# Layer one's output weights on one core: storing the converted value, or its two halves

## The chip, the core and the metric

The program runs on one core of one Trainium2 chip. The metric is device time in microseconds (us) of one execution. All inputs are float32, except that three weight arrays arrive as the words of float64 values and are converted on the chip.

## The reference

```python
# attention: 4 x 8 heads, 576 positions, head size 64, causal window 128, linear bias
scores = scale * np.matmul(q, k.transpose(0, 1, 3, 2))
scores = np.where(mask, scores + bias[None], -1000000000.0)
...
x = attn_out                                  # 2304 tokens x 512
# layer one, 1536 hidden units
g = x @ w_gate
x = (g * sigmoid(g) * (x @ w_val)) @ w_out    # the change concerns w_out here
# layer two, 2048 hidden units
h = x @ w_in
y = (h * np.tanh(softplus(h))) @ w_out
```

## The kernel before

TensorE multiplies in a format narrower than float32, so each operand is kept as two halves: `hi`, a copy rounded to that format (ScalarE, `hi_act`, L121), and `lo`, the rest (VectorE, `lo_dve`, L124). A product is three matmuls: hi by hi, hi by lo, lo by hi.

**Layer one** runs over five chunks of tokens (512, 384, 512, 512, 384). While chunk `ci` goes through layer one, the attention of chunk `ci+1` is mixed in. Per chunk there are 12 blocks `i` of 128 hidden units: `gv_groups` (L651) makes the gate and value products and the halves `hh`, `hl` of the activation, and `out_group` (L684) multiplies those by the block's output weights into four PSUM accumulators `acc0` to `acc3` (`proj`, L628: 12 matmuls). In the first four chunks `out_group` runs one block behind `gv`; in the last chunk (number 4) six behind, so that its last six output groups stand one after another at the end of layer one, with no other matmul between them.

**The ring.** The output weights come in six pieces `r` of two blocks. A piece lies as a tile `ring` [128, 2, 1024] (both halves, 1 MB); there are two such buffers, so piece r can enter only when the output groups of piece r-2 have been multiplied. In chunk 0 `conv_ring` (L489) converts a piece from float64 words (`convert`, L416), keeps the converted float32 value in a tile `cw` (512 KB), stores that to device memory (`w1od`), and makes the two halves. Chunks 1 to 4 call `load_ring` (L506), 24 times in all: it loads the float32 value back into a `cw` buffer and makes the halves again, one ScalarE and one VectorE instruction.

**Background.** Conversions, splits and loads are steps in a queue `bg`; `pump` issues some after every group. `conv_w2` (L520) converts layer two's weights in chunks 1 to 3 and spaces its blocks by a `pause` that it works out from the number of calls. In chunk 4 `combos` (L561) splits eight blocks of layer two's second weights and stores 1.8 MB for each.

**Layer two** starts on TensorE right after layer one's last output group. Its tokens are split into parts `xs1` to `xs7` (VectorE and ScalarE, from `xr`), and for each block j of two hidden tiles `make_win` (L817) makes a weight tile `win`: GpSimd forms four differences into a single buffer `t4` (L822), ScalarE the hi part, VectorE the lo part, in two instructions each, one from the raw block `w4` and one from `t4`. `hidden` (L833) multiplies seven groups of six matmuls per block j in the order 1, 6, 7, 5, 2, 4, 3; group 2 goes on in the bank of group 1, and group 3 in that of group 5. `bank()` (L712) gives the groups alternately a rotating bank and one of `acc0` to `acc3`; group 1 of the first block gets a rotating one and group 6 `acc1`. Layer one's results leave the accumulators through `evacuate` (L635): `acc0` and `acc2` by ScalarE (L638), `acc1` and `acc3` by VectorE (L639), into tiles `ev`.

**Order.** TensorE's order is the order of the program. On the other engines and in SyncE's DMA queue a scheduler sets the order when the kernel is built; each then runs strictly in that order.

Of the kernel before, what the change touches and what calls it, by code (L numbers as in the profile page):

```python
# [9 lines left out]
F32 = mybir.dt.float32  # L10
# [12 lines left out]
NF1, NF2 = F1 // 128, F2 // 128  # L23
# [69 lines left out]
def body(ctx: ExitStack, tc: tile.TileContext, qT, kT, vP, w1, w1o, w2, cst, yT):  # L93
    nc = tc.nc
# [4 lines left out]
    hp_ = sa.enter_context(tc.tile_pool(name="hp", bufs=2, side="right"))  # L99
    dr = ctx.enter_context(tc.tile_pool(name="dr", bufs=1, space=bass.MemoryType.DRAM))  # L100
    ps = ctx.enter_context(tc.tile_pool(name="ps", bufs=4, space=bass.MemoryType.PSUM))

    x2d = dr.tile([128, CT, NT], F32, name="x2d")
    w1od = dr.tile([NF1 // 2, 128, 1024], F32, name="w1od")
    w2d = dr.tile([NF2, 128, 1024], F32, name="w2d")
    w2o = dr.tile([7, 128, NJ, 2, 256], F32, name="w2o")
    cst_sb = const.tile([128, 452], F32, name="cst_sb")
# [12 lines left out]
    def hi_act(out, in_):  # L120
        return nc.scalar.activation(out=out, in_=in_, func=AF.Copy)  # L121

    def lo_dve(out, in_, hi):
        return nc.vector.tensor_tensor(out=out, in0=in_, in1=hi.bitcast(F32), op=ALU.subtract)  # L124
# [175 lines left out]
    last_of = {}  # L300
    behind = []
# [87 lines left out]
    wt, ring, spill = {}, {}, {}  # L389
    bg = collections.deque()  # L390
# [17 lines left out]
    def steps(key, fs, front=False):  # L408
        if front:
            bg.extendleft([(key if f is fs[-1] else None, f) for f in fs][::-1])  # L410
            return
        for f in fs[:-1]:
            bg.append((None, f))
        bg.append((key, fs[-1]))
# [36 lines left out]
    def halves(st, alloc, put):  # L451
        def f1():
            st["h"] = alloc()
            hi_act(st["h"][:, 0], st["w"])

        def f2():
            lo_dve(st["h"][:, 1], st["w"], st["h"][:, 0])
            put(st["h"])

        return [f1, f2]  # L460
# [4 lines left out]
    def ring_tile():  # L465
        return hp_.tile([128, 2, 1024], F32R, tag="ring", name="ring", bufs=2)

    stage = {}
# [20 lines left out]
    def conv_ring(r):  # L489
        st = {}  # L490

        def spill_it():
            nc.sync.dma_start(out=w1od[r], in_=st["w"])

        def put(w):
            ring[0, r] = w
            stage.pop(("o", r))
            if r + 1 < NF1 // 2:
                stage_other(("o", r + 1), w1o[r + 1])

        steps(
            ("ring", 0, r),
            convert(stage["o", r], st) + [spill_it] + halves(st, ring_tile, put),
        )

    def load_ring(ci, r):  # L506
        st = {}

        def f0():
            st["w"] = hp_.tile([128, 1024], F32, tag="cw", name="cw")  # L510
            nc.sync.dma_start(out=st["w"], in_=w1od[r])

        def put(w):
            ring[ci, r] = w

        steps(
            ("ring", ci, r), [f0, lambda: None] + halves(st, ring_tile, put), True
        )

    def conv_w2(blocks, calls):  # L520

        pause = max(6, (calls - 24 - 9 * len(blocks)) // len(blocks))

        def wait(n):
            for _ in range(n):
                bg.append((None, lambda: None))

        def block(i, after):
            st, raw = {}, {}

            def run(k):
                if not raw:
                    raw["f"] = convert(stage.pop(("2", i)), st)
                raw["f"][k]()

            def put():
                nc.sync.dma_start(out=w2d[i], in_=st["w"])

            for k in (0, 2, 3):
                bg.append((None, lambda k=k: run(k)))  # L540
                wait(1)
            if after is not None:
                bg.append((None, lambda: stage_other(("2", after), w2[after])))
            bg.append((None, lambda: run(1)))
            bg.append((None, lambda: run(4)))
            bg.append((None, put))
            wait(pause)

        bg.append((None, lambda: stage_other(("2", blocks[0]), w2[blocks[0]])))
        wait(pause)  # L550
        for i, after in zip(blocks, blocks[1:] + [None]):
            block(i, after)
# [406 lines left out]
    with tc.manual_schedule(engines={mybir.EngineType.PE}):  # L959
# [45 lines left out]
        for ci, p in enumerate(plansA):  # L1005
# [36 lines left out]
            for gi, (kind, i, f) in enumerate(groups):  # L1042
                if ci == 0 and kind == "gv" and gi % 3 == 0:
                    if 0 < i < NF1 - 2:
                        conv_w1(i + 2)
                    if i == 0:
                        conv_ring(1)
                        bg.insert(len(bg) - 4, (None, lambda: behind.append(last_of["x", 3])))
                f()
                if ci or not win:  # L1050
                    pump(CFG["pump_g"])
                elif gi % 3 == 0:
                    due = max(1, -(-len(bg) // 4))
                if not ci:
                    pump(due)
                while win and (spent * ng < (gi + 1) * total or gi == len(groups) - 1):
                    _, cost, e = win.popleft()
                    e()
                    spent += cost
                    pump(CFG["pump_p"] if ci else due)  # L1060
# [76 lines left out]
```

## Time and profile before

| | |
|---|---|
| median of 3 runs | 956.66 us (956.12 to 958.75) |
| the profiled execution | 955.31 us |
| its span in the trace | 953.4 us |
| TensorE busy | 924.4 us, 97% of the span |
| VectorE busy | 702.4 us, 74% |
| ScalarE busy | 524.5 us, 55% |
| GpSimd busy | 204.9 us, 21% |
| DMA queue of SyncE | 173.94 MB, 55.4% of 16 engines' span |

In the profile PE is TensorE, DVE VectorE, ACT ScalarE, POOL GpSimd and SP SyncE. A busy TensorE hides little: a microsecond taken from another engine shortens the run only where TensorE waits for that engine. The places where it waits are therefore what to look for, and the clock it is granted after each wait.

### The profile page before, as it was taken

What the parts mean: (1) busy time and instruction counts of PE and PEld (TensorE: products, weight loads), DVE (VectorE), ACT (ScalarE), POOL (GpSimd) and SP (SyncE); (2) the same over time, 40 slices, a digit from 0 to 9 for tenths busy, and PEclk for the clock granted to TensorE, in tenths of its full rate; (3) what the DMA queues carried; (4) which work ended last, traced back from release to release, by engine and by line L of the source; (5) the groups of instructions that cost most, each with busy time, mean ns of one, the idle gap of its engine ahead of it and who ended that gap; (6) DMA issues with size and microseconds to landing.
All of it is one profiled execution on the core that took longest, in us unless ns stands there. A gap on an engine that the chain in (4) does not pass through costs nothing. (4 is left out here: it accounts for less than half of the span.)

```text
span 953.4 us, 14622 instructions
## 1 busy us (share of the span) xinstructions
PE 924.4 (97%) x5040; PEld 832.0 (87%) x5040; DVE 702.4 (74%) x1341; ACT 524.5 (55%) x1135; POOL 204.9 (21%) x332
## 2 busy tenths in 40 slices
PE   6998999999999999999999998999999999999998
PEld 4766777899988888888889998899999999999997
DVE  6899997687866866567565668788877878677673
ACT  6766667666575655445534445555545555355442
POOL 0314223110210332010113325542012420132000
PEclk9999999999999999999999999999999999999999
DMA  9855434376636554165348993525793257830385
GB/s 305 294 202 197 167 91 126 97 228 198 216 94 202 167 186 134 51 206 168 132 147 284 375 327 101 210 70 193 252 307 110 77 184 261 301 118 4 103 266 183
DMA packets 76921, 174.86 MB, mean 183 GB/s; under 512 B 9136, under 2 KB 52528, under 8 KB 67120
## 3 DMA queue, kind: packets, MB, share of 16 engines
q1 hardware_dynamic: 76848, 173.94, 55.4%
q8 instruction: 40, 0.66, 0.3%
q14 instruction: 33, 0.27, 0.1%
HBM read 138.25 MB, written 35.65 MB: 182 GB/s over the span
## 5 line engine op out<-in xcount | busy, mean ns | idle before, releaser
L114 PE MATMUL g_ps<-xt,w 128*128 128x512 f32 (+1 forms) x1440 | 317.4, 373 | 0.6 <-DVE t L661 0.6
L114 PEld LDWEIGHTS g_ps<-xt,w 128*128 128x128 f32 x1440 | 257.7, 188 | 36.4 <-issue 2.3
L114 PE MATMUL bk<-xs,win 128*128 128x384 f32 x1008 | 180.1, 338 | 5.5 <-DVE G L726 4.9
L114 PEld LDWEIGHTS bk<-xs,win 128*128 128x128 f32 x1008 | 176.0, 189 | 9.2 <-DVE G L726 8.0
L114 PE MATMUL bk<-op,wout 128*128 128x384 f32 x1008 | 175.8, 335 | 0.6 <-DMA wout<-w2o 0.6
L114 PEld LDWEIGHTS bk<-op,wout 128*128 128x128 f32 x1008 | 174.8, 188 | 1.1 <-issue 1.1
L114 PE MATMUL acc<-hh,ring 128*128 128x512 f32 (+1 forms) x480 | 151.6, 379 | 1.9 <-DVE ring L124 1.8
L121 ACT ACTIVATE op<-G 128x768 fp32r<-128x768 f32 x84 | 70.8, 846 | 65.6 <-PE bk L114 63.0
L114 PEld LDWEIGHTS acc<-hh,ring 128*128 128x128 f32 x480 | 91.4, 193 | 15.2 <-DVE ring L124 2.6
L268 POOL TENSOR_SCALAR_AFFINE_SELECT PT<-PT 128x256 f32<-128x256 f32 (+4 forms) x80 | 51.8, 662 | 240.3 <-ACT PT L265 240.1
L124 DVE TENSOR_TENSOR op<-G,op 128x768 fp32r<-128x768 f32 x84 | 79.6, 955 | 26.9 <-ACT op L121 26.3
L822 POOL TENSOR_TENSOR t<-w 128x256 f32<-128x256 f32 x48 | 43.3, 921 | 224.6 <-DVE win L124 206.3
L114 PE MATMUL acc<-hl,ring 128*128 128x512 f32 (+1 forms) x240 | 90.2, 376 | 0.8 <-DVE hl L124 0.8
L237 ACT ACTIVATE Pt<-Pt,sm 128x128 f32<-128x128 f32 (+1 forms) x160 | 62.4, 391 | 17.1 <-DVE sm L233 16.1
L726 DVE TENSOR_TENSOR G<-u,bk 128x384 f32<-128x384 f32 x72 | 39.0, 553 | 31.8 <-PE bk L114 29.7
L121 ACT ACTIVATE hh<-t 128x512 fp32r<-128x512 f32 (+1 forms) x60 | 35.0, 583 | 47.0 <-DVE t L669 46.8
L1081 ACT ACTIVATE G<-G 128x384 f32<-128x384 f32 x72 | 36.8, 519 | 42.2 <-DVE G L726 42.2
L660 ACT ACTIVATE t<-g_ps 128x512 f32<-128x512 f32 (+1 forms) x60 | 32.7, 546 | 45.8 <-PE g_ps L114 45.6
L661 DVE SCALAR_TENSOR_TENSOR t<-t,g_ps 128x512 f32<-128x512 f32 (+1 forms) x60 | 37.6, 626 | 27.0 <-ACT t L660 26.9
L252 ACT ACTIVATE Pt<-Pt,sm 128x128 f32<-128x128 f32 (+1 forms) x144 | 46.3, 391 | 12.4 <-DVE sm L248 12.2
L114 PEld LDWEIGHTS acc<-hl,ring 128*128 128x128 f32 x240 | 46.3, 193 | 6.2 <-DVE hl L124 1.1
L124 DVE TENSOR_TENSOR hl<-t,hh 128x512 fp32r<-128x512 f32 (+1 forms) x60 | 39.8, 663 | 15.2 <-ACT hh L121 14.6
(78 smaller groups left out, 1235.1 us busy)
## 6 DMA issues: line engine op xcount, KB each, us to landing
wout<-w2o SPq DMA_DIRECT2D x42, 1024.0 KB, 6.1
wraw<-w SPq DMA_DIRECT2D x16, 1024.0 KB, 5.8
w2o<-chl SPq DMA_DIRECT2D x16, 896.0 KB, 9.0
wst<-w SPq DMA_DIRECT2D x12, 1024.0 KB, 6.9
cw<-w1od SPq DMA_DIRECT2D x24, 512.0 KB, 4.3
w<-w2d SPq DMA_DIRECT2D x24, 512.0 KB, 3.3
w2d<-cw SPq DMA_DIRECT2D x16, 512.0 KB, 5.0
wraw<-w1o SPq DMA_DIRECT2D x6, 1024.0 KB, 5.1
```

The lines of the kernel that those rows point to most:

```text
L114: nc.tensor.matmul(out=out, lhsT=lhsT, rhs=rhs, start=start, stop=stop, skip_group_check=True)
L121: return nc.scalar.activation(out=out, in_=in_, func=AF.Copy)
L124: return nc.vector.tensor_tensor(out=out, in0=in_, in1=hi.bitcast(F32), op=ALU.subtract)
L237: nc.scalar.activation(out=Pt[:q.qn], in_=Pt[:q.qn], func=AF.Exp, scale=-1.0, bias=sm[:q.qn, i:i + 1], accum_out=sm[:q.qn, 8 + i:9 + i],)
L252: last_of["exp"] = nc.scalar.activation(out=pt, in_=pt, func=AF.Copy, scale=r)
L268: nc.gpsimd.affine_select(out=here, in_=prev, pattern=[[0, m], [1, n]], compare_op=ALU.is_ge, fill=0.0, base=0, channel_multiplier=-1,)
L660: tanhs.append(nc.scalar.activation(out=t[:, :n], in_=st["g"][:, :n], func=AF.Tanh, scale=0.5))
L661: nc.vector.scalar_tensor_tensor(out=t[:, :n], in0=t[:, :n], scalar=1.0, in1=st["g"][:, :n], op0=ALU.add, op1=ALU.mult)
L726: nc.vector.tensor_tensor(out=out, in0=a, in1=b, op=op)
L822: nc.gpsimd.tensor_tensor(out=x[:, o], in0=a, in1=b, op=ALU.subtract)
L1081: nc.scalar.activation(out=out, in_=in_, func=AF.Mish)
```

## The change

The DRAM array takes both halves of a piece. `conv_ring` stores the finished ring tile after its lo half, in place of the float32 value after the conversion. `load_ring` becomes one step with one DMA of 1 MB straight into the ring tile; its ScalarE and VectorE instructions and its `cw` buffer go. The spacing of `conv_w2` and the place of one inserted step are adapted to the shorter queue.

```diff
-    w1od = dr.tile([NF1 // 2, 128, 1024], F32, name="w1od")
+    w1od = dr.tile([NF1 // 2, 128, 2, 1024], F32, name="w1od")
...
     def conv_ring(r):
         st = {}
 
-        def spill_it():
-            nc.sync.dma_start(out=w1od[r], in_=st["w"])
-
         def put(w):
             ring[0, r] = w
+            nc.sync.dma_start(out=w1od[r], in_=w.bitcast(F32))
             stage.pop(("o", r))
...
-            convert(stage["o", r], st) + [spill_it] + halves(st, ring_tile, put),
+            convert(stage["o", r], st) + halves(st, ring_tile, put),
...
     def load_ring(ci, r):
-        st = {}
-
         def f0():
-            st["w"] = hp_.tile([128, 1024], F32, tag="cw", name="cw")
-            nc.sync.dma_start(out=st["w"], in_=w1od[r])
-
-        def put(w):
-            ring[ci, r] = w
-
-        steps(
-            ("ring", ci, r), [f0, lambda: None] + halves(st, ring_tile, put), True
-        )
+            ring[ci, r] = ring_tile()
+            nc.sync.dma_start(out=ring[ci, r].bitcast(F32), in_=w1od[r])
+
+        steps(("ring", ci, r), [f0], True)
 
     def conv_w2(blocks, calls):
 
-        pause = max(6, (calls - 24 - 9 * len(blocks)) // len(blocks))
+        pause = max(6, (calls - 7  - 10 * len(blocks)) // (len(blocks) + 1))
...
-                        bg.insert(len(bg) - 4, (None, lambda: behind.append(last_of["x", 3])))
+                        bg.insert(len(bg) - 3, (None, lambda: behind.append(last_of["x", 3])))
```

TensorE's order stays as it was. The scheduler's order of the other engines changes in many places; three matter here.

The first is VectorE at the passage from layer one to layer two. `win_6106`, `win_6117` and `win_6220` are the weight tiles of blocks 0, 1 and 2 of layer two before; `w4` is a raw block and `t4` GpSimd's differences. Before:

```order
L124 TENSOR_TENSOR ring_6174<-cw_6172,ring_6174 128x1024
L124 TENSOR_TENSOR win_6117<-w4_6082,win_6117 128x768
L124 TENSOR_TENSOR xs7_6075<-xr_5421,xs7_6075 128x768
L726 TENSOR_TENSOR xr_5421<-xr_5421 128x2x384
L124 TENSOR_TENSOR win_6106<-t4_6074,win_6106 128x1024
L124 TENSOR_TENSOR xs6_6079<-xr_5421,xs6_6079 128x768
L124 TENSOR_TENSOR win_6220<-w4_6111,win_6220 128x768
L639 COPY ev_6201<-acc1_5765 128x384
L124 TENSOR_TENSOR xs3_6081<-xr_5421,xs3_6081 128x768
L639 COPY ev_6205<-acc3_5767 128x384
L124 TENSOR_TENSOR win_6117<-t4_6074,win_6117 128x1024
L726 TENSOR_TENSOR u_6235<-u_6235,bk_6237 128x384
```

The same place in the changed kernel, where blocks 0, 1 and 2 have the tiles `win_6037`, `win_6048` and `win_6148`:

```order
L124 TENSOR_TENSOR win_6048<-w4_6013,win_6048 128x768
L124 TENSOR_TENSOR win_6037<-t4_6005,win_6037 128x1024
L124 TENSOR_TENSOR xs3_6012<-xr_5364,xs3_6012 128x768
L124 TENSOR_TENSOR win_6148<-w4_6042,win_6148 128x768
L124 TENSOR_TENSOR win_6048<-t4_6005,win_6048 128x1024
L630 COPY ev_6129<-acc1_5716 128x384
L630 COPY ev_6133<-acc3_5718 128x384
L124 TENSOR_TENSOR win_6148<-t4_6005,win_6148 128x1024
L717 TENSOR_TENSOR u_6163<-u_6163,bk_6165 128x384
L717 TENSOR_TENSOR u_6180<-u_6163,bk_6173 128x384
L717 TENSOR_TENSOR G_6155<-u_6180,bk_6182 128x384
```

The ring instructions are gone. The evacuations of `acc1` and `acc3` (now L630) stood ahead of block 1's lo part from `t4`, and stand behind it; block 2's stood behind the first `u` and `G`, and stands ahead of them.

The second is SyncE's DMA queue at the same passage. `cw<-w1od` (before) and `ring<-w1od` (now) bring pieces 4 and 5 of the last chunk, `w4<-w2d` layer two's raw blocks. Before:

```order
L511 DMA cw_6063<-w1od_73 128x1024
L591 DMA w2o_75<-chl_5885 128x7x256
L591 DMA w2o_75<-chl_5888 128x7x256
L511 DMA cw_6172<-w1od_73 128x1024
L591 DMA w2o_75<-chl_5928 128x7x256
L591 DMA w2o_75<-chl_5949 128x7x256
L815 DMA w4_6072<-w2d_74 128x1024
L815 DMA w4_6082<-w2d_74 128x1024
L815 DMA w4_6111<-w2d_74 128x1024
```

Now, with piece 3 at the top:

```order
L507 DMA ring_5903<-w1od_73 128x2048
L582 DMA w2o_75<-chl_5819 128x7x256
L582 DMA w2o_75<-chl_5840 128x7x256
L806 DMA w4_6003<-w2d_74 128x1024
L806 DMA w4_6013<-w2d_74 128x1024
L507 DMA ring_5997<-w1od_73 128x2048
L507 DMA ring_6103<-w1od_73 128x2048
L806 DMA w4_6042<-w2d_74 128x1024
```

Pieces 4 and 5 were asked for ahead of the last stores of `combos`; they now follow the first two raw blocks of layer two.

The third is VectorE late in chunk 0, ahead of `Q_1462`, an attention operand that TensorE waits for. Before:

```order
L124 TENSOR_TENSOR w_1535<-cw_1516,w_1535 128x1024
L445 SCALAR_TENSOR_TENSOR cw_1589<-cw_1589,cp_1587 128x1024
L233 ISA Pt_1419,sm_1411<-s_ps_1410,cst_sb_76 128x128
L233 ISA sm_1411 128x1
L233 ISA Pt_1422,sm_1411<-s_ps_1410,cst_sb_76 64x128
L233 ISA sm_1411 64x1
L434 TENSOR_SCALAR cw_1666<-wst_1147 128x1024
...
L124 TENSOR_TENSOR KL_1464<-kraw_1299,K1_1463 128x512
L193 SCALAR_TENSOR_TENSOR Q_1462<-qraw_1298,Q_1462 64x384
L439 SCALAR_TENSOR_TENSOR cw_1666<-wst_1147,cw_1666 128x1024
```

Now:

```order
L434 TENSOR_SCALAR cw_1666<-wst_1147 128x1024
...
L652 SCALAR_TENSOR_TENSOR t_1441<-t_1441,g_ps_1428 128x512
L124 TENSOR_TENSOR KL_1464<-kraw_1299,K1_1463 128x512
L439 SCALAR_TENSOR_TENSOR cw_1666<-wst_1147,cw_1666 128x1024
L193 SCALAR_TENSOR_TENSOR Q_1462<-qraw_1298,Q_1462 64x384
L233 ISA Pt_1421,sm_1413<-s_ps_1412,cst_sb_76 128x128
L233 ISA sm_1413 128x1
L233 ISA Pt_1424,sm_1413<-s_ps_1412,cst_sb_76 64x128
L233 ISA sm_1413 64x1
```

A conversion step (L439) moved from behind `Q_1462` to ahead of it, and two score reductions (L233, each with its read-out) from ahead of it to behind it.

## Rows read from the trace of the kernel before

**Rows 1.** Busy time by stretch (us; PE, PEld, DVE, ACT, POOL; PEclk, DMA share, GB/s)
```profile
160.00:260.00 100.00, 99.81 (x626) 93.19 (x624) 75.60 (x186) 64.68 (x169) 16.48 (x30) 1.00 0.57 173
260.00:360.00 100.00, 99.25 (x556) 82.69 (x557) 69.28 (x188) 62.53 (x188) 21.46 (x56) 1.00 0.54 166
...
460.00:560.00 100.00, 100.00 (x535) 90.25 (x534) 64.53 (x101) 44.28 (x80) 29.20 (x38) 1.00 0.73 253
```

**Rows 2.** Waits of TensorE: us in total, times, longest
```profile
PE acc L114 <- DVE ring L124: 1.8, 1, 1.8
```

**Rows 3.** The ring tile's two split instructions: ns min/median/max, first and last start
```profile
L121 ACT ACTIVATE ring<-cw x30: 1042/1057/1062, 21.8 to 576.5; 128x1024 fp32r<-128x1024 f32 x30
L124 DVE TENSOR_TENSOR ring<-cw,ring x30: 1192/1225/1766, 24.1 to 581.9; 128x1024 fp32r<-128x1024 f32 x30
```

**Rows 4.** Timeline of TensorE, the last output groups: start, us, operation [idle before]
```profile
571.94 0.51 PE L114 MATMUL acc<-hh,ring 128*128 128x384 f32 x2
...
583.15 0.62 PE L114 MATMUL acc<-hh,ring 128*128 128x384 f32 x2 [1.80 <-DVE ring L124]
...
588.67 4.35 PE L114 MATMUL bk<-xs,win 128*128 128x384 f32 x24
```

**Rows 5.** Timeline of VectorE, same passage
```profile
575.10 1.77 DVE L124 TENSOR_TENSOR ring<-cw,ring 128x1024 fp32r<-128x1024 f32 x1
...
581.89 1.21 DVE L124 TENSOR_TENSOR ring<-cw,ring 128x1024 fp32r<-128x1024 f32 x1
...
585.63 1.21 DVE L124 TENSOR_TENSOR win<-t,win 128x1024 fp32r<-128x1024 f32 x1
...
588.50 0.54 DVE L639 COPY ev<-acc 128x384 f32<-128x384 f32 x1
...
593.21 1.23 DVE L124 TENSOR_TENSOR win<-t,win 128x1024 fp32r<-128x1024 f32 x1 [2.76 <-ACT win L121]
```

**Rows 6.** Timeline of SyncE's DMA queue, the first two raw blocks of layer two
```profile
566.98 1.54 SPq L815 DMA_DIRECT2D w<-w2d  x2
```

**Rows 7.** Tile wout after 600 us, 39 loads of 1024 KB
```profile
DMA to landing us min/median/max: 4.9/5.8/9.1
```

**Rows 8.** Timeline of GpSimd, the differences of blocks 1 and 2
```profile
586.92 3.67 POOL L822 TENSOR_TENSOR t<-w 128x256 f32<-128x256 f32 x2 [6.63 <-DVE win L124]
...
594.52 1.43 POOL L822 TENSOR_TENSOR t<-w 128x256 f32<-128x256 f32 x2 [2.43 <-DVE win L124]
```

**Rows 9.** Timeline of TensorE in layer two, two runs of 84 matmuls
```profile
613.55 16.41 PE L114 MATMUL bk<-xs,win 128*128 128x384 f32 x84 [2.00 <-DVE G L726]
630.55 14.84 PE L114 MATMUL bk<-xs,win 128*128 128x384 f32 x84 [0.59 <-DVE G L726]
```

**Rows 10.** Groups of the page: two of VectorE's instructions in layer two (busy, mean ns)
```profile
L124 DVE TENSOR_TENSOR op<-G,op 128x768 fp32r<-128x768 f32 x84 | 79.6, 955 | 26.9 <-ACT op L121 26.3
...
L726 DVE TENSOR_TENSOR G<-u,bk 128x384 f32<-128x384 f32 x72 | 39.0, 553 | 31.8 <-PE bk L114 29.7
```

**Rows 11.** Timeline of VectorE late in chunk 0
```profile
139.74 0.28 DVE L233 CUSTOM_DVE_ANT_0 Pt<-s_ps,cst_sb 128x128 f32<-128x128 f32 x1
...
143.13 0.55 DVE L193 SCALAR_TENSOR_TENSOR Q<-qraw,Q 64x384 fp32r<-64x384 f32 x1
143.72 1.23 DVE L439 SCALAR_TENSOR_TENSOR cw<-wst,cw 128x1024 f32<-128x1024 uint32 x1
```

**Rows 12.** Timeline of TensorE, its last two waits in chunk 0
```profile
119.90 0.58 PE L114 MATMUL s_ps<-K,Q 128*128 128x256 f32 x1 [1.53 <-DVE Q L193]
...
143.74 0.38 PE L114 MATMUL s_ps<-K,Q 128*128 128x256 f32 x1 [1.15 <-DVE Q L193]
```

**Rows 13.** Two stretches behind a wait of TensorE, as in rows 1
```profile
583.00:588.00 5.00, 4.85 (x19) 4.85 (x20) 5.00 (x7) 1.75 (x3) 1.08 (x1) 0.66 0.01 4
...
143.70:148.00 4.30, 4.26 (x23) 3.60 (x24) 4.28 (x11) 3.06 (x7) 3.69 (x6) 1.00 0.63 210
```

**Rows 14.** DMA from 540 to 600 us, GB/s in 40 slices of 1.5 us
```profile
GB/s 380 384 360 348 384 344 359 292 334 359 394 395 388 386 288 134 265 384 386 293 258 341 246 33 5 0 0 93 257 0 0 0 0 245 17 96 286 443 431 366
```

## The prediction

> **What bounds the kernel now.** I read the busy times by stretch first. In the middle of layer one TensorE is busy 99.3 to 100 us of every 100 at full clock, and its gaps in the 300 us shown add up to 0.94 us [rows 1]; VectorE is at 65 to 76 there, ScalarE at 44 to 65. Work that leaves those two engines in layer one's middle buys next to nothing. Then came TensorE's list of waits: for the ring's lo half it waits once in the whole run, 1.8 us [rows 2]. So the place to read closely is the passage from layer one to layer two, 570 to 615 us, with the new orders of VectorE and SyncE beside the timelines; after that late chunk 0, where VectorE's order moved ahead of an operand that TensorE waits for [rows 12]. About 0.3% (2.9 us) is what a measurement of this kernel can tell from no change.
>
> **The change part by part.**
>
> *The splits that go.* 24 of the 30 ScalarE copies of 1.057 us and 24 of the 30 VectorE subtractions of 1.225 us [rows 3] disappear: 25 us of ScalarE, 29 us of VectorE. All but the last two lie under a busy TensorE and are worth zero; the cover is TensorE's own work, which stays. The last two subtractions are those at 575.10 and 581.89 us [rows 5].
>
> *More bytes.* Each of 24 loads grows from 0.5 to 1 MB, each of six stores by 0.5 MB: 15 MB on 174. The DMA share in layer one's middle is 0.54 to 0.73 [rows 1], so there is room. A 1 MB load lands in 4.9 to 9.1 us, median 5.8 [rows 7]. It can start only when the output groups of piece r-2 are through. The shortest time from there to the need, but for the last two pieces, is in the last chunk: two hidden blocks and two output groups, 72 matmuls. 84 take 14.84 us at full clock [rows 9], so 72 take 12.7. That hides 9.1. Cost zero.
>
> *The last two pieces.* Here only two output groups lie between, 24 matmuls or 4.2 us. Group 6 begins at 572.1 (inside the first of [rows 4]); that frees piece 4's buffer. Landing 4.9 to 5.8 later gives 577.0 to 577.9; the need is at 576.3. New wait: 0.7 to 1.6 us, in place of 1.80. Piece 5's buffer is free at 576.3, the piece lands at 581.2 to 582.1 and is needed 4.2 after piece 4 came: no wait. Six groups take 12.7 us, so layer one would end at 585.5 to 586.4, or up to 1.7 later if the clock falls behind the wait (it was 0.66 over 5 us behind the present one [rows 13]). Before, it ended at 588.67 [rows 4]. I take 586.0, without the fall. The queue should not hold these loads back: the two raw blocks now ahead of them went out at 567 to 568.5 [rows 6].
>
> The Trainium skill (DMA: Bandwidth & Descriptors, Anatomy of one DMA) fits a DMA's time as 2.0 us plus its bytes over 436 GB/s; for 1 MB that is 4.4 us, an estimate from that page. By it the new wait would be 0.2 us and layer one would end at 585.0, which speaks for the change. The rows, at 4.9 and more, disagree, and the sum goes by them.
>
> *The evacuation.* This gain meets a new gate. Group 6 of layer two's first block is multiplied into `acc1`, so it waits for VectorE's evacuation of `acc1`. That copy ran at 588.50 [rows 5], ahead of block 1's lo part; now it stands behind it, and VectorE takes its queue in order. When is that lo part done? Before: block 0's lo part from `t4` started at 585.63, GpSimd began block 1's differences when it ended (586.92), and block 1's lo part ran from 593.21 to 594.44 [rows 5, 8]. In the new order two ring subtractions (1.77 and 1.21 us) no longer stand ahead of block 0's lo part, but one more `xs` of the size 128x768, 0.96 us [rows 10], does: 1.9 us earlier, less the overlaps. GpSimd took 3.67 us for two differences beside a full VectorE and 1.43 beside a lighter one [rows 8]; fewer instructions now run beside it, and I give it 0.5 us back. Block 1's lo part then ends at 592.0 and the copy of 0.54 us at 592.5. Group 6 began at 589.7 before (588.67 plus six matmuls); now it begins at 592.5, after a wait of 5.4 us behind group 1, which is all that TensorE has to do.
>
> *What is late next.* From 592.5 five groups of 1.06 us, 1.6 us for a fallen clock (below) and group 3 put block 1's start on TensorE at 600.4. In the trace TensorE waits 2.00 us, until 613.55, for an addition of block 2 behind VectorE's backlog [rows 9]; that is its seventh group. In the new order TensorE reaches this group 78 matmuls after 600.4, at 614.2. VectorE's queue from 600.4 on: the last addition of block 0, block 3's two lo parts (they need block 0's buffer and ScalarE's hi parts) until 604.4; block 1's five additions and one `op`, the last of which follow TensorE, until 608.8; then a sum of 128x768, block 4's two lo parts, another sum, two `u` and the addition in question: three instructions of 128x768 at 0.96, one of 128x1024 at 1.2, three at 0.55 [rows 5, 10], with GpSimd beside them some 0.6 more: 615.2. TensorE goes on at 615.2, 1.65 late, after a wait of 1.0 instead of 2.00.
>
> *The clock.* Behind the wait of 2.00 us, 84 matmuls took 16.41 us, against 14.84 in the next run [rows 9]: 1.57 lost. Behind 1.80 the granted clock was 0.66; behind 1.15 it was 1.00 [rows 12, 13]. The nearest row to a wait of 1.0 is the one with 1.15, so I count 1.57 as saved. The passage then nets +1.65 - 1.57 = +0.1 us. Bounds: -2.7 (evacuation not in the way, 588.67 - 586.0 kept) and +2.8 (592.5 - 589.7, nothing comes back).
>
> *Late chunk 0.* `Q` ran at 143.13 on VectorE and TensorE waited 1.15 us for it [rows 11, 12]. A conversion step of 1.23 us moves ahead of it, two reductions of 0.28 move behind: 0.7 later. TensorE's next work follows this wait directly, so +0.7. Bounds: -0.5 (the other moves in this chunk) and +2.3 (the wait passes 1.53, and 1.57 is lost to the clock as in layer two). I take +0.7, because the wait at 119.90 [rows 12] grows by about 0.3 in the same way, which takes as much off this one.
>
> *The rest.* The background queue loses three steps per load and the pause is worked out anew; TensorE has almost no wait there to gain or lose [rows 1]. TensorE's order, and layer two from 615 us on, stay.
>
> Sum: 0 + 0.1 + 0.7 = +0.8 us on the profiled execution's 955.31 (span 953.4, 1.9 around it), 956.1. That execution is 1.35 below the median of the runs shown; on the median, 956.66, the forecast is 957.5 us, with a range of its own of 956 to 959.
>
> **The rivals.**
>
> *The backlog decides (slower).* Until 560 us the DMA engines move 288 to 395 GB/s, and they go quiet only at 574.5 [rows 14]. The stores of `combos`, the ring pieces and layer two's first raw blocks share that backlog; piece 3 now puts 0.5 MB more ahead of the raw blocks, 1.4 us at 380. If the first raw block lands that much later, GpSimd's differences, the lo parts, the evacuation and the addition of block 2 all come 1.4 later: TensorE goes on at 616.6, waits 2.4, and the clock falls as now: +1.65 + 1.4 + 0.7 = +3.75, 960.4 us. It decides once the raw block is about half a microsecond late, where the wait leaves the 1.15 of [rows 12] behind. For it: the slices at 380 and above. Against it: pieces 4 and 5 leave this stretch, so the bytes before 572 us hardly grow.
>
> The Trainium skill (DMA: Bandwidth & Descriptors, Specifications) gives one core about 358 GB/s of device memory; the slices up to 560 us lie around that figure, and a stretch at its ceiling is what this rival needs.
>
> *Both clocks fall (slower).* The waits stay as forecast, but the clock falls behind 1.0 and 1.5 us too: +0.8 + 1.57 + 1.57 = +3.9, 960.6 us.
>
> *The evacuation is not in the way (faster).* If block 1's lo part is done by 587 us, layer one's gain is kept and the wait of 2.00 with its clock goes: -2.7 - 1.57 + 0.7 = -3.6, 953.1 us. It needs GpSimd and VectorE 5 us earlier than worked out.
>
> *Ring loads late in every chunk (slower).* If SyncE's queue holds a load back by 7 us or more (12.7 less 5.8), each such piece costs the excess; five pieces at 2 us are +10, 967 us. The order shows few long waits next to these loads.
>
> *No effect at all.* The order shows all 24 splits gone from both engines; the change does what it says.
>
> **How the numbers follow.** Forecast 0.52; backlog 0.22; both clocks 0.12; evacuation free 0.09; late loads 0.05. Of the forecast's 0.52 I count 0.02 past the bound as slower. Of the 0.34 of the two slower rivals just past it, 0.09 as inside; of the faster one 0.02. So faster 0.07, same 0.61, slower 0.32. The range leaves out the late loads, the lower part of the faster rival and what exceeds the slower ones by 2 us: 954.0 to 962.5.
>
> **What would show it.** Right: `acc<-hh,ring` waiting about 1 us once, for a DMA; layer two's first group soon after 586, then a wait of some 5 us released by an `ev`; 613.55 becoming about 615; chunk 0's last wait near 1.6. Wrong: no wait at the evacuation, a wait for ring in several chunks, or a gain or loss of more than 1 us between 160 and 560 us.

## The result, and the profile after

The changed kernel takes 964.26 us, the median of six runs from 961.29 to 967.07. The kernel before took 957.01 us in its six. The ratio is 1.0071, with a 95% interval of 1.0050 to 1.0093: the change makes the kernel slower by 0.7%, about 7 us. The forecast was 957.5 us with a range that ended at 962.5, so it was too low by 7.

The profiled execution took 967.07 us, with a span of 965.4 where before had 953.4: 12.0 more. First the page of the changed kernel, with the engines' busy times and the queue of the loads.

```profile
PE 925.6 (96%) x5040; PEld 833.6 (86%) x5040; DVE 670.9 (70%) x1317; ACT 502.8 (52%) x1111; POOL 191.6 (20%) x332
...
q1 hardware_dynamic: 76848, 189.66, 58.6%
```

VectorE has 31.5 us less to do than before (702.4) and ScalarE 21.7 less (524.5), and 15.7 MB more are moved. The work went as the change says. The time was lost elsewhere. Four rows of TensorE cut the span into pieces: the wait that ends chunk 0, the last hidden block of layer one, and a run of 84 matmuls in layer two. The timeline of the kernel before has the second of them here; its first and third stand in [rows 12] and [rows 9].

```profile
565.85 4.33 PE L114 MATMUL g_ps<-xt,w 128*128 128x384 f32 x24
```

The same timeline of the changed kernel:

```profile
142.90 0.36 PE L114 MATMUL s_ps<-K,Q 128*128 128x256 f32 x1 [1.58 <-DVE Q L193]
...
578.20 4.33 PE L114 MATMUL g_ps<-xt,w 128*128 128x384 f32 x24
...
590.52 0.41 PE L114 MATMUL acc<-hh,ring 128*128 128x384 f32 x1 [1.74 <-DMA ring<-w1od]
...
598.92 1.22 PE L114 MATMUL bk<-xs,win 128*128 128x384 f32 x6
604.95 21.82 PE L114 MATMUL bk<-xs,win 128*128 128x384 f32 x114 [4.81 <-DVE ev L630]
627.65 14.86 PE L114 MATMUL bk<-xs,win 128*128 128x384 f32 x84 [0.89 <-DVE G L717]
642.72 14.86 PE L114 MATMUL bk<-xs,win 128*128 128x384 f32 x84 [0.21 <-DVE G L717]
```

Up to the end of chunk 0 the changed kernel is 0.84 us early (142.90 against 143.74). From there to the last hidden block it takes 435.30 us instead of 422.11: 13.19 more. From that block to the second run of 84 matmuls it takes 64.52 instead of 64.70, and the rest is level. So the whole loss lies between 143 and 578 us, in the middle of layer one, and not in the passage that the prediction was about. I call this stretch, from the last wait of chunk 0 to the last hidden block, the middle, and read it in the same way in every trace below.

The busy times by stretch of the changed kernel, columns as in [rows 1]:

```profile
160.00:260.00 100.00, 94.55 (x573) 87.82 (x572) 64.57 (x171) 55.77 (x155) 12.74 (x28) 0.97 0.64 204
260.00:360.00 100.00, 96.55 (x540) 81.65 (x539) 62.99 (x172) 55.52 (x169) 15.19 (x54) 1.00 0.60 193
```

TensorE, which had gaps of 0.94 us there [rows 1], now stands for 5.45 and 3.45 us in these two stretches; from 360 to 560 us it is full as before. Its waits from 160 to 560 us (in total, times, longest) add up to the same 8.9:

```profile
PE s_ps L114 <- DVE Q L193: 5.0, 2, 2.8
PE o_ps L114 <- issue: 3.2, 2, 2.6
PE g_ps L114 <- DVE sm L233: 0.7, 1, 0.7
```

For the waits of `o_ps` the profile names no releaser (`issue`); what they are for is not shown. The kernel before had 0.94 us of waits in its middle, so 8.0 of the 13.19 us are new ones. The other 5.2 are the same matmuls running longer. The whole middle, before and then changed, columns as above:

```profile
143.74:565.85 422.11, 421.16 (x2337) 366.39 (x2337) 285.99 (x642) 234.53 (x589) 84.31 (x164) 1.00 0.57 183
142.90:578.20 435.30, 426.40 (x2337) 370.44 (x2338) 258.55 (x623) 215.41 (x571) 72.86 (x163) 0.99 0.62 203
```

Most of these 5.2 us are clock. Two of the stretches behind such a stop, at 219.64 and 242.45:

```profile
219.00:226.00 7.00, 6.36 (x38) 5.57 (x39) 6.57 (x19) 5.95 (x18) 0.10 (x1) 0.76 0.97 378
242.00:247.00 5.00, 4.55 (x20) 4.55 (x21) 4.58 (x13) 2.75 (x8) 0.90 (x1) 0.67 0.97 406
```

Behind the third long stop, at 357.76, the granted clock was 0.73 from 357.7 to 364, with 5.54 us busy. By these three rows the lost clock is 0.24 of 6.36 us, 0.33 of 4.55 and 0.27 of 5.54, an estimate of 4.5 us in all.

What released TensorE at 242.45? The chain of waits, followed back from the program's end, runs through this place (start, us, what; it shows only pieces of the chain):

```profile
206.92 8.16 DMA wraw<-w
...
215.11 0.69 DVE cw L434
...
219.31 8.28 DMA ring<-w1od
...
241.71 0.70 DVE Q L193
...
242.45 0.74 PE s_ps L114 x4
```

A raw block of layer two's weights (`wraw`) is 8.16 us under way. Its conversion (`cw`) stands on VectorE, and what is queued behind it is late. The chain also runs through a ring load of 8.28 us; the experiments on the bytes and on the queue take that up. A conversion begins with `cw` on VectorE and `cg` on ScalarE, which both read the raw block, and `cp` on VectorE reads `cg`. The waits of VectorE and ScalarE for raw blocks, 146 to 570 us of the changed kernel, were the next thing to read:

```profile
DVE cw L434 <- DMA wraw<-w: 23.8, 11, 4.4
DVE cp L427 <- ACT cg L422: 6.7, 3, 6.0
...
ACT cg L422 <- DMA wraw<-w: 30.0, 11, 6.6
```

The kernel before also waited for raw blocks, and in total longer (its timeline, 146 to 570 us):

```profile
DVE cp L427 <- ACT cg L422: 33.7, 15, 6.6
...
ACT cg L422 <- DMA wraw<-w: 37.6, 16, 7.3
```

So the sum of these waits explains nothing. What differs is what stands behind them. VectorE around one and the same `Q`, first in the kernel before, where the conversion beside it is that of the fourth of the 16 raw blocks:

```profile
232.18 0.29 DVE L233 CUSTOM_DVE_ANT_0 Pt<-s_ps,cst_sb 128x128 f32<-128x128 f32 x1
...
233.77 0.43 DVE L427 TENSOR_SCALAR cp<-cg 128x512 int32<-128x512 int32 x1 [1.29 <-ACT cg L422]
234.39 0.82 DVE L124 TENSOR_TENSOR KL<-kraw,K 128x640 fp32r<-128x640 f32 x1 [0.20 <-ACT K L121]
235.25 0.69 DVE L193 SCALAR_TENSOR_TENSOR Q<-qraw,Q 64x512 fp32r<-64x512 f32 x1
235.97 0.69 DVE L434 TENSOR_SCALAR cw<-wraw 128x1024 int32<-128x1024 int32 x1
```

and in the changed kernel, where it is that of the fifth:

```profile
237.70 0.69 DVE L434 TENSOR_SCALAR cw<-wraw 128x1024 int32<-128x1024 int32 x1 [3.88 <-DMA wraw<-w]
...
240.44 0.82 DVE L124 TENSOR_TENSOR KL<-kraw,K 128x640 fp32r<-128x640 f32 x1
241.17 0.28 DVE L233 CUSTOM_DVE_ANT_0 Pt<-s_ps,cst_sb 128x128 f32<-128x128 f32 x1
...
241.71 0.69 DVE L193 SCALAR_TENSOR_TENSOR Q<-qraw,Q 64x512 fp32r<-64x512 f32 x1
```

Before, the `cw` at this place stands behind `KL` and `Q`, the operands of the next scores. Now one stands ahead of them, and ahead of one group's softmax (L233). ScalarE begins the same operands, and its `cg` stands ahead of `K` and `Q` in both kernels. Before and then changed:

```profile
232.61 1.12 ACT L422 ACTIVATE cg<-wraw 128x1024 bf16<-128x1024 bf16 x1 [1.51 <-DMA wraw<-w]
237.69 1.18 ACT L422 ACTIVATE cg<-wraw 128x1024 bf16<-128x1024 bf16 x1 [3.17 <-DMA wraw<-w]
```

`K` followed at 233.64 and at 238.78. The block had been issued at 226.87 before; now it is the next block, issued at 231.53. The conversions also follow their loads more closely: for the second to the fifth block, `cw` starts 11.5, 9.9, 9.1 and 12.3 us after the load is issued before, and 8.5, 8.2, 6.0 and 6.2 in the changed kernel.

### The profile page after: what moved, and what is told of

Its sections match the earlier page's. It is cut to its first block, busy times and chain, and to the rows that moved or that the text cites. A ratio compares the mean times of both kernels' runs of the same rounds, so it can differ in the third digit from the quotient of the medians.

```text
span 965.4 us, 14556 instructions
## 1 busy us (share of the span) xinstructions
PE 925.6 (96%) x5040; PEld 833.6 (86%) x5040; DVE 670.9 (70%) x1317; ACT 502.8 (52%) x1111; POOL 191.6 (20%) x332
## 4 chain that ended last, share of the span: by engine, by line
PE 79%; DVE 11%; DMA 5%; issue 2%; ACT 2%; SPq 1%; POOL 1%; DVEq 0%; ACTq 0%; POOLq 0%
PE bk L114 33%; PE g_ps L114 27%; PE acc L114 12%; PE o_ps L114 3%; PE s_ps L114 3%; DMA wraw<-w 2%; PE t_ps L259 1%; DVE G L717 1%; DVE cw L445 1%; DMA wst<-w 1%; DMA ring<-w1od 1%; DVE cw L439 1%; DVE Pt L233 1%; DVE win L124 1%; DMA w2d<-cw 1%
## 5 line engine op out<-in xcount | busy, mean ns | idle before, releaser
L268 POOL TENSOR_SCALAR_AFFINE_SELECT PT<-PT 128x256 f32<-128x256 f32 (+4 forms) x80 | 46.5, 596 | 261.6 <-ACT PT L265 261.4
L652 DVE SCALAR_TENSOR_TENSOR t<-t,g_ps 128x512 f32<-128x512 f32 (+1 forms) x60 | 37.7, 629 | 52.3 <-ACT t L651 52.3
L660 DVE SCALAR_TENSOR_TENSOR t<-t,g_ps 128x512 f32<-128x512 f32 (+1 forms) x60 | 37.8, 630 | 32.3 <-PE g_ps L114 31.8
```

The costliest lines, as they stand in the source:

```text
L268: nc.gpsimd.affine_select(out=here, in_=prev, pattern=[[0, m], [1, n]], compare_op=ALU.is_ge, fill=0.0, base=0, channel_multiplier=-1,)
L652: nc.vector.scalar_tensor_tensor(out=t[:, :n], in0=t[:, :n], scalar=1.0, in1=st["g"][:, :n], op0=ALU.add, op1=ALU.mult)
L660: nc.vector.scalar_tensor_tensor(out=t[:, :n], in0=t[:, :n], scalar=0.5, in1=vps[:, :n], op0=ALU.mult, op1=ALU.mult)
```

## The experiments

Three theories. **Bytes:** the second 0.5 MB of each ring load makes raw blocks land late. **Order:** with the splits gone the scheduler puts the conversions in other places among the attention steps, and there their waits hold up operands of TensorE. **Queue:** a ring load that waits for its buffer holds up SyncE's queue. All results in one table; "middle" is the stretch defined above, 422.1 us before and 435.3 in the changed kernel, in the one profiled execution of each.

| kernel | median us (range) | ratio to before, 95% interval | middle us |
|---|---|---|---|
| again | 962.38 (961.42 to 965.3) | 1.0056 (1.0038 to 1.0075) | 433.3 |
| half_bytes | 964.14 (961.33 to 966.26) | 1.0070 (1.0050 to 1.0090) | 437.8 |
| before_more_bytes | 963.2 (961.18 to 964.22) | 1.0061 (1.0042 to 1.0081) | 427.8 |
| pool_queue | 974.33 (967.97 to 979.04) | 1.0181 (1.0149 to 1.0214) | 445.9 |
| dummy_splits | 964.99 (963.1 to 967.93) | 1.0069 (1.0046 to 1.0092) | 427.1 |
| pinned | 953.46 (951.47 to 954.18) | 0.9943 (0.9922 to 0.9963) | 420.8 |
| pinned_slow_pace | 955.31 (952.79 to 956.88) | 0.9971 (0.9956 to 0.9986) | 422.0 |
| before_pinned | 956.19 (954.1 to 959.81) | 0.9979 (0.9964 to 0.9994) | 421.5 |
| pinned_dve | 959.47 (955.72 to 961.18) | 1.0027 (1.0016 to 1.0039) | 428.8 |
| pinned_act | 953.66 (952.54 to 956.19) | 0.9966 (0.9955 to 0.9978) | 421.9 |
| no_raw_loads | 951.56 (950.97 to 954.49) | 0.9948 (0.9934 to 0.9963) | 420.8 |
| pinned_ev_first | 953.92 (950.65 to 959.02) | 0.9975 (0.9959 to 0.9991) | 427.1 |

**again**: no edit.

> The changed kernel once more, unedited, as the yardstick of this group. Its six times so far lie in two groups, 961.3 to 962.2 and 966.4 to 967.1 us. All theories expect 961 to 967. If the cause is one or two stalls of TensorE that happen or do not happen (each 2.6 to 2.9 us long in the trace, and a lower granted clock behind it), the profile of an execution near 961 lacks one of the stalls at 219.64, 242.45 or 357.76 that the profile of 967.07 shows.

The slowdown repeats. The profiled execution, 965.3 us, stops at the first two places again with other sizes, 1.52 us at 219.38 and 4.71 at 242.47; at 333.86 it stops for 2.84 (0.58 in the first), at 358 not at all. So the sizes change from one execution to the next. That the landing of the blocks sets them is likely, but not shown. No execution near 961 was profiled, so what such a one lacks stays untested.

**half_bytes**

```diff
-            nc.sync.dma_start(out=ring[ci, r].bitcast(F32), in_=w1od[r])
+            nc.sync.dma_start(out=ring[ci, r][:, 0].bitcast(F32), in_=w1od[r, :, 0])
...
-            mm(acc[c][:, :n], w[:, 1, lo:lo + 128], hh[:, :n], False, last)
+            mm(acc[c][:, :n], w[:, lo_at, lo:lo + 128], hh[:, :n], False, last)
```

> The changed kernel, but a later chunk loads only the hi half (0.5 MB, as many bytes as the load of the kernel before) and TensorE multiplies by it a second time in place of the lo half: the same matmuls, the correction by the lo half is left out of chunks 1 to 4. The order of the engines stays nearly that of the changed kernel. Theory of the bytes (the second 0.5 MB of each load delays the raw blocks of the background conversions, whose first VectorE and ScalarE steps then block both queues): about 957 us, the stalls at 219, 242 and 358 us gone. Theory of the order (with the splits gone the conversions stand closer together and in other places among the attention steps, whatever the DMA does): stays at 961 to 966, and the stalls stay. Theory of the queue (the load waits at the head of SyncE's queue for its slot): stays at 961 to 966.

The theory of the bytes falls for this kernel: with the bytes of before it is as slow. VectorE at the same place as above:

```profile
236.38 0.70 DVE L434 TENSOR_SCALAR cw<-wraw 128x1024 int32<-128x1024 int32 x1 [6.62 <-DMA wraw<-w]
...
241.11 1.00 DVE L193 SCALAR_TENSOR_TENSOR Q<-qraw,Q 64x512 fp32r<-64x512 f32 x1
```

SyncE issued this block at 228.51, VectorE had reached its conversion at 229.76, and TensorE stood 6.59 us for the `Q` behind it.

**before_more_bytes**

```diff
             nc.sync.dma_start(out=st["w"], in_=w1od[r])
+            if ci < last:
+                dm = bpool["a"].tile([128, 1024], F32, tag="dm", name="dm", bufs=1)
+                nc.sync.dma_start(out=dm, in_=w1od[r])
```

> The kernel before, with a second load of 0.5 MB of the same stored piece into a tile that nobody reads, behind each load of chunks 1 to 3 (so the bytes of the changed kernel, with the splits and the order of before). Theory of the bytes: slower by 3 to 9 us, 960 to 966, with stalls of TensorE between 160 and 560 us behind a raw block. Theory of the order: 957, within 0.3%.

This speaks for the bytes: 5.6 us in the middle, with stops of 2.36 us (`Q`, 217.61) and 2.68 us (250.71). Taken together with the run before, neither theory is whole. In nearly the order of before (one `cw`, at 226.89, now stands ahead of a `Q` that it followed) the bytes cost 5.6 us; in the order of the change taking them away gains nothing. It looks as if the order of before had so little room behind its raw blocks that either change uses it up.

**pool_queue**

```diff
-            nc.sync.dma_start(out=ring[ci, r].bitcast(F32), in_=w1od[r])
+            nc.gpsimd.dma_start(out=ring[ci, r].bitcast(F32), in_=w1od[r])
```

> The changed kernel, with the loads of the ring issued from GpSimd's DMA queue, so that nothing on SyncE waits behind them. Theory of the queue: 957 us, with SyncE's loads of q, k, v and the raw blocks earlier. Theory of the bytes and theory of the order: no change, 961 to 967; the bytes are the same and the raw blocks share the same engines.

Slower by another 10 us, which no theory expected. In the changed kernel a ring load waits only once for long at the head of SyncE's queue between 160 and 360 us, 2.8 us, so there was little to free:

```profile
SPq L507 <- PE acc L114: 2.8, 1, 2.8
```

The theory of the queue falls: with the ring loads out of SyncE's queue, the raw block ahead of the stop near 242 us went out at 232.75, no earlier than in the changed kernel (231.53). GpSimd's waits in this kernel, 146 to 570 us:

```profile
POOL ring L507 <- PE acc L114: 84.7, 17, 14.2
```

The load now waits for its buffer at the head of GpSimd's queue, 17 times and up to 14.2 us, and GpSimd's masks of `PT` stand in the same queue. But from each of TensorE's four longest stops (5.86, 3.29, 3.18 and 2.27 us) the chain of waits leads to a raw block and not to a mask, so why this run is slower still is open.

**dummy_splits**

```diff
+        def d1():
+            st["d"] = hp_.tile([128, 1024], F32R, tag="cw", name="cw")
+            hi_act(st["d"], ring[ci, r][:, 0].bitcast(F32))
+
+        def d2():
+            lo_dve(st["d"], ring[ci, r][:, 0].bitcast(F32), st["d"])
+
-        steps(("ring", ci, r), [f0], True)
+        steps(("ring", ci, r), [f0, lambda: None, d1, d2], True)
```

> The changed kernel, with the 24 ScalarE copies and 24 VectorE subtractions put back as work that nobody reads: behind each load one copy of 128x1024 into a cw tile and one subtraction on it, as steps of the background queue and with the cw buffer, as in the kernel before. Loads, stores and bytes are those of the changed kernel. Theory of the order (with the splits gone the scheduler draws the conversion's first steps nearer to the issue of their raw block, so VectorE and ScalarE stand idle at the head of their queues until it lands, and the attention steps behind them reach TensorE late): faster by 3 to 7 us than the changed kernel although it does more, about 957 us, the stalls of over 2 us at 219, 242 and 334 to 358 us gone. Theory of the bytes: no gain, 961 to 967, or slower by the work put back.

The time did not move, where about 957 had been expected, but the middle did: 427.1 instead of 435.3, with one stop of 2.95 us left. Work that nobody reads made the middle 8 us shorter, and VectorE's waits of `cw` for a raw block fell to nothing:

```profile
DVE cw L434 <- DMA wraw<-w: 0.2, 1, 0.2
```

At the place read above it is the order of before again, `cw` behind `Q`:

```profile
239.37 0.69 DVE L193 SCALAR_TENSOR_TENSOR Q<-qraw,Q 64x512 fp32r<-64x512 f32 x1
...
243.19 0.69 DVE L434 TENSOR_SCALAR cw<-wraw 128x1024 int32<-128x1024 int32 x1
```

What is left, 5.0 us over before, is about the 5.6 of before_more_bytes; that it is the same price is not shown. The run puts back two things at once, the splits and the three queue steps per load, and does not tell which of them moves the conversions. The gain went into a new wait: TensorE stood 8.09 us at 590.16 for a ring piece. pinned_slow_pace, below, has a like one, and both put the three steps per load back.

**pinned**, **pinned_slow_pace**, **before_pinned**: one order is added to the changed kernel, to it with three empty steps per load, and to the kernel before.

```diff
-            nc.vector.reciprocal(out=sm[:, 16:16 + nb_], in_=sm[:, 8:8 + nb_])
+            last_of["rec"] = nc.vector.reciprocal(out=sm[:, 16:16 + nb_], in_=sm[:, 8:8 + nb_])
...
-                raw["f"][k]()
+                with tc.issue_after(last_of["act"].ins), tc.issue_after(last_of["rec"].ins):
+                    raw["f"][k]()
```

> The changed kernel, with one order added: the steps of a background conversion of layer two's weights may stand on ScalarE and VectorE only behind the newest attention step issued by then (the last copy of PT, the last reciprocal). No work is added or taken away and the raw block's load is left free to go early. Theory of the order: the waits of VectorE for a raw block (cw, 23.8 us in 11 waits between 146 and 577 us in the changed kernel) fall to under half, TensorE's stalls of over 2 us between 160 and 460 us go, 956 to 959 us. Theory of the bytes: raw blocks land as late as before, and the time stays at 961 to 967.

> As the pinned kernel, and the three empty steps behind each load are put back in the background queue, so that it runs as slowly as in the kernel before. Theory of the order: as pinned or a little better, 955 to 959. If pinned gains and this loses, the pace, not the place beside attention, is what matters; theory of the bytes: 961 to 967.

> The kernel before, with the same order added. Its TensorE has next to no stall in layer one's middle, so the theory of the order expects no change within 0.3%, 955 to 959; slower by more would say that the added order itself costs something.

The order decides. By the medians pinned is 10.8 us faster than the change (964.26), with the same work and the same bytes, and faster than the kernel before; 956 to 959 had been expected. Its TensorE does not wait once between 160 and 560 us, and the clock stays up:

```profile
160.00:260.00 100.00, 100.00 (x630) 93.79 (x629) 69.09 (x189) 61.78 (x175) 14.34 (x30) 1.00 0.62 202
```

Its VectorE around the same `Q`:

```profile
232.32 0.82 DVE L124 TENSOR_TENSOR KL<-kraw,K 128x640 fp32r<-128x640 f32 x1
233.17 0.69 DVE L193 SCALAR_TENSOR_TENSOR Q<-qraw,Q 64x512 fp32r<-64x512 f32 x1
...
237.69 0.69 DVE L434 TENSOR_SCALAR cw<-wraw 128x1024 int32<-128x1024 int32 x1 [2.94 <-DMA wraw<-w]
```

The raw block, issued at 229.18, lands 8.5 us later; the one at this place in the changed kernel took 6.2 (231.53 to 237.69). VectorE waits 2.94 us for it, but `KL` and `Q` are through, and TensorE notices nothing. The slow pace adds nothing to this and takes a little: its conversions end later, and the stores of `combos` and layer two's first raw blocks are still going out when pieces 4 and 5 of the ring are due, and TensorE waits 7.64 us for one of them. SyncE's queue in pinned_slow_pace:

```profile
562.45 7.20 SPq L583 DMA_DIRECT2D w2o<-chl  x3
569.71 4.33 SPq L807 DMA_DIRECT2D w<-w2d  x2
574.14 1.37 SPq L507 DMA_DIRECT2D ring<-w1od  x2
```

In pinned the same two ring loads went out from 570.94. The order gives the kernel before less (0.9979), as expected within 0.3%. By the medians the change with the order is 2.7 us ahead of before with the order; the two profiled executions have the same span, 952.5 us, so where these 2.7 us lie is not shown.

**pinned_dve**, **pinned_act**: the order of pinned on one engine alone.

```diff
-                with tc.issue_after(last_of["act"].ins), tc.issue_after(last_of["rec"].ins):
+                with tc.issue_after(last_of["rec"].ins):
```

(and the other half alone for pinned_act)

> The pinned kernel with the order on VectorE alone; ScalarE's conversion step (cg) is free to stand early. If VectorE's place decides, 953 to 956; if ScalarE's, 961 to 967.

> The pinned kernel with the order on ScalarE alone; VectorE's first conversion step (cw) is free to stand early, though the fifth step cannot run before ScalarE's. If ScalarE's place decides, 953 to 956; if VectorE's, 959 to 967, with VectorE's waits of cw for a raw block still there.

ScalarE's place gives nearly all: 953.66. VectorE's place alone gives 4.8 us (959.47 against 964.26), a time between the two ranges expected. With ScalarE's order alone VectorE still waits 17.0 us for raw blocks, 9 times, up to 3.8, and TensorE stops once, 1.01 us. With VectorE's order alone ScalarE keeps 29.1 us of waits, up to 6.7, and TensorE stands 4.95 us for `Q` at 241.79. `Q` and `K` begin on ScalarE, so an early `cg` there holds up VectorE's half of them too: at that stop `cg` waited 6.70 us up to 238.42, and `KL` waited 7.09 for `K`. The two engines are not separated cleanly, since with ScalarE's order alone `cw` has left its place ahead of this `Q` as well (`Q` at 234.86, the next `cw` at 248.32).

**no_raw_loads**

```diff
-                bg.append((None, lambda: stage_other(("2", after), w2[after])))
+                bg.append((None, lambda: stage.update({("2", after): raw["t"]})))
```

> The changed kernel, but in each chunk only the first raw block of layer two's weights is loaded and converted over again in place of the others: 13 of the 16 conversions of layer two's weights have no load, the rest of the work stands. It leaves the other blocks' weights out. Theory of the order, as a wait: VectorE and ScalarE no longer stand idle at the head of their queues, the stalls of over 2 us between 200 and 460 us go, last block of layer one at 564 to 567 us instead of 577 to 578, time 952 to 956. If instead the conversions' own 4 us of VectorE work ahead of the attention operands is the price, the stalls stay and the time is 961 to 966.

All conversions run, at the early places of the changed kernel and earlier, but most without a block to wait for: TensorE has no wait from 160 to 560 us and the time is 951.56. The order was drawn anew here too: five `cw` stand by 215.56 us, where the changed kernel had three, and none near the stop at 242. So early conversions without a wait cost nothing that shows; it is the wait for the landing that costs. This run also moves 13.6 MB less, but half_bytes showed that fewer bytes alone give nothing here.

**pinned_ev_first**

```diff
+                    if p == 0 and j == 1 and src is x:
+                        es.enter_context(tc.issue_after(last_of["evA"].ins))
+                        es.enter_context(tc.issue_after(last_of["evD"].ins))
...
-        next(second)
         for f in carry:
             f()
+        next(second)
```

> The pinned kernel, and the evacuation of layer one's last sums stands on ScalarE and VectorE ahead of the lo part of block 1 instead of behind it (the last output groups are issued first, and block 1's second half is ordered behind the evacuation). It tests the evacuation gate of the prediction: in the pinned kernel TensorE waits 5.27 us for the copy of acc1 and the 114 matmuls behind it take 22.77 us, where 114 at full clock take 20.1. If that gate is the whole price, this gains 5 to 7 us, 947 to 949. If VectorE's backlog is late next (the addition at 614.56, where TensorE already waits 0.54), most of it comes back as a longer wait there: the 5.27 shrinks to under 1, the wait before 614 to 616 grows to 2 to 4, and the time gains 1 to 3 us, 950.5 to 952.5.

No gain to be measured (953.92 against 953.46), where 947 to 952.5 had been expected. TensorE in pinned, and then here:

```profile
591.25 22.77 PE L114 MATMUL bk<-xs,win 128*128 128x384 f32 x114 [5.27 <-DVE ev L631]
614.56 14.85 PE L114 MATMUL bk<-xs,win 128*128 128x384 f32 x84 [0.54 <-DVE G L718]
```

```profile
591.79 3.36 PE L114 MATMUL bk<-xs,win 128*128 128x384 f32 x18 [0.57 <-DVE ev L631]
...
617.40 16.17 PE L114 MATMUL bk<-xs,win 128*128 128x384 f32 x84 [3.59 <-DVE G L718]
```

The gate opens, 5.27 becomes 0.57, and the addition behind VectorE's backlog becomes late in its place: 0.54 becomes 3.59, and the 84 matmuls behind it lose 1.3 us to the clock. The profiled execution, 959.02 us, was the slowest of twelve and also shows that the pin is no full cure: one raw block kept VectorE 7.2 us, and TensorE stood 3.75 us at 245.46.

## Why the prediction was wrong

**The step that failed is "The rest".** It said that the background queue changes but that "TensorE has almost no wait there to gain or lose", from a TensorE that is 99.3 to 100% busy [rows 1]. A busy engine has nothing to gain. That it has nothing to lose was a false step: the row says nothing of how late its operands may come. The profiled pair lost 13.19 us there against 12.0 in the whole: 8.0 are new waits, and 5.2 are the same matmuls running longer, mostly by the clock behind the waits. The prediction had named the sign, "a gain or loss of more than 1 us between 160 and 560 us", but gave the case no chance. The cause, conversions that wait for a raw block ahead of TensorE's operands, is shown from three sides: free the operands from the wait (pinned, 953.46), take the wait away (no_raw_loads, 951.56), or put the splits back (dummy_splits, middle 8 us shorter). Which part of the change draws the conversions to these places stays open: dummy_splits put back the splits and the queue steps together, and no run takes up the new `pause` alone.

The Trainium skill (PSUM — Partial Sum Buffer, Engine vs sequencer instructions) calls the queues of ScalarE, VectorE and GpSimd strictly first in, first out. The trace agrees: VectorE stood idle for 3.88 us up to 237.70 and ScalarE for 3.17 up to 237.69, each with its steps of `K` and `Q` queued behind; in pinned VectorE ran `KL` and `Q` at 232.32 and 233.17.

**The removed splits, worth zero**: right about the engines' busy time, wrong as a whole, since the change moved what stands beside them. "The cover is TensorE's own work, which stays" looked only at the work that goes.

**More bytes, cost zero**: right in the changed kernel's order, by half_bytes; with the order pinned no cost of them shows either (953.46, and 956.19 for before_pinned). The landing was 4.2, 5.3 and 9.2 us (shortest, median, longest), inside the 12.7 of cover. Wrong in nearly the order of before, where they cost 5.6 us through the raw blocks, which the step did not look at.

**The last two pieces and the evacuation**: right within 0.6 us. Shifted by the 12.35 us that the last hidden block is late, the wait for the piece is 1.74 us (0.7 to 1.6 said, so just outside), layer one ends at 586.57 (586.0), group 6 begins at 592.60 (592.5) after 4.81 us of waiting (5.4). The fit of a DMA's time that the prediction takes from the Trainium skill (DMA: Bandwidth & Descriptors, Anatomy of one DMA) stands there for DMAs that GpSimd issues. The ring's loads are SyncE's, and at 5.3 us in the median they took longer than its 4.4.

**What is late next, and the clock**: right. The addition comes at 615.30 (615.2), the wait is 0.89 (1.0), and the 84 matmuls behind it take 14.86 us, so 1.55 of the 1.57 us came back. The passage nets -0.2 (+0.1 said). pinned_ev_first shows the order of what is late next too.

**Late chunk 0**: the wait came out at 1.58 (1.55 or so was said), but the wait at 119.90 shrank to 0.49 instead of growing, and chunk 0 ended 0.84 early in this execution and level in the repeated run (143.73). The +0.7 of the sum did not come.

**The rivals**: "Ring loads late in every chunk" had the time of the upper runs, 967, by another mechanism: TensorE waits for a ring piece once, 1.7 us, as forecast. The backlog and the two clocks did not come. The 358 GB/s that the prediction takes from the Trainium skill (DMA: Bandwidth & Descriptors, Specifications) is no ceiling here: slices of [rows 14] reach 443.

## What to carry to other kernels

A busy share of 99% on the bounding engine says that nothing is to be gained beside it, and nothing about what can be lost: for each operand that it needs, look at which instruction stands ahead of it in its producer's queue and whether that one waits for a transfer. When a change removes instructions from a kernel whose order a scheduler draws, the rest is drawn anew; compare where the transfer-fed steps stand before and after, and keep them behind the newest work that the bounding engine waits for. Here one added order was worth 10.8 us and turned the change from a loss of 0.7% into a gain of 0.6%.

## What had not been expected of the hardware

Stops of 2.6 and 2.8 us inside an otherwise full TensorE brought the granted clock to 0.76 and 0.67 over the 7 and 5 us around them. Over the whole middle the same matmuls took 5.2 us longer than before, beside 8.9 us of stops; in the repeated run it was 3.1 us beside 9.1. Behind the longest stop, 6.59 us in half_bytes, the granted clock was at its lower level, 1.2 GHz, for the whole 4 us that follow:

```profile
242.00:246.00 4.00, 3.83 (x13) 3.83 (x14) 2.94 (x15) 3.40 (x11) 0.61 (x1) 0.50 0.99 335
```
